# The places of ScalarE's and GpSimd's share in converting the weights, in a fused attention and feed-forward kernel

## The chip, the cores and the metric

The kernel runs on one core of a Trainium2 chip. The core has a matrix engine (TensorE, PE in the profile; its weight loads are PEld), three engines for elementwise work (VectorE or DVE, ScalarE or ACT, GpSimd or POOL), and a queue that issues transfers (SyncE, SP). Each engine works through its own instructions in the order in which the program gives them, and waits for others by semaphores. The metric is the device time of one execution in microseconds (us). Times of several executions are given as a median. One further execution was recorded by the profiler.

## What is computed

```python
def _attn_ref(q, k, v, tau):
    scores = scale * np.matmul(q, k.transpose(0, 1, 3, 2))
    thresh = np.max(scores, axis=-1, keepdims=True) - tau
    scores = np.where(scores >= thresh, scores, -1000000000.0)
    ...
    attn = attn / (np.sum(attn, axis=-1, keepdims=True) + 1e-09)
    return np.matmul(attn, v)
...
    xn = (x - mu) / np.sqrt(var + 1e-06) * g_ln
    ch = np.maximum(xn @ w_ch1, 0.0) @ w_ch2
    return (x + ch)
```

There are 8 batches, 8 heads, 576 positions and 64 features per head. A softmax keeps only the scores within tau of the row's largest. The heads side by side make the 512 features of the second half, a normalisation and a feed-forward network of 2048 hidden features. The two weight matrices, w_ch1 (512 x 2048) and w_ch2 (2048 x 512), arrive as 64-bit floating point numbers, while q, k and v are 32-bit. Converting those weights on the chip is what the change is about.

## The kernel before

**Attention.** The work goes in 72 stages (n), nine per batch. Stage n takes two heads with half of their 512 first queries, or, in the fifth stage of a batch, the 64 last queries of all heads. It makes four blocks of 128 queries by 576 keys: the scores on PE (L422, into sc), their row maxima on DVE (L436), exponentials on ACT (L450, two pairs, one per half of sc), and on DVE the product with the mask (score at least threshold), which also sums the rows (L457). The reciprocal of these sums (L464, L462) is applied in one of two ways. In stages 0 to 5 ACT writes it into diagonal matrices (L471), and PE multiplies the blocks by them and turns them in the same step (tp, tr), which ACT copies out (L507, L501, L530). From stage 6 on (FIRST) POOL scales the blocks (L473), DVE turns them by 32 x 32 blocks into et (L547), and two transfers through memory (scr, L554; em, L568) put them in place. PE then multiplies by the values (L616, L626), and ACT copies the result to x (L639). In stages 1 to 4 PE is also given some products of constants (warm) ahead of the scores.

**Feed-forward.** Each batch gives two groups of 288 tokens. A group's first layer has 16 steps d: 16 matmul records of 128 x 288 into one of two banks of PSUM in turn, then ACT's relu (L814), which frees the bank. Group 0 runs its second layer plainly; its matmuls appear as p at L101, as those of the first layer do. Later groups use a scheme with seven products for eight (seg). The generator of these steps is drawn on by second_part, four times in a stage, so that PE's order is attention and feed-forward in fixed alternation.

**The conversion.** The weights are cut into 32 chunks of 128 x 512: 0 to 15 are w_ch1, four for each quarter of the hidden features, and 16 to 31 are w_ch2. A chunk is fetched raw (two 32-bit words for a number) into a free place. Then
- begin (DVE, L273 and L277) takes sign, exponent and upper mantissa from the upper word into the chunk;
- ScalarE converts the lower word to its top bits (here called the convert, L283), and squares the upper word, taken as a 32-bit number, in place (the square, L286). The square overwrites what begin reads;
- carry (POOL, L296) adds the converted word to the chunk as an integer;
- mask (DVE, L302) compares the square with a constant and multiplies the chunk by the result; it frees the raw place;
- scale (POOL, L312) multiplies a chunk of w_ch1 by g_ln.

A step of the first layer needs the four scaled chunks of its quarter, one of the second layer the masked chunk.

**What sets the order.** It is written out by hand in the loop over n. The table BEGUN says how many chunks shall have been begun at three places of stage n: at masks_at (after the second pair of exponentials), at behind_at (after the L457s) and at end_at (at the end of the stage). In stages 1 to 5 two places are used: one chunk is begun at masks_at and one at end_at. From stage 6 on two or three are begun at masks_at and as many at behind_at. The two ScalarE operations of a chunk are put on one list, on_scalar, by begin, as a pair. They are given to ACT by flush: all at once in carry_all, or one after each relu of the first layer. mask_all masks every carried chunk; it is called ahead of the begins at masks_at and ahead of those at behind_at. The lines of the loop that matter, shortened (next(rest, None) gives the second pair of exponentials):

```python
        next(rest, None)
        ...
        conversion.mask_all()
        conversion.begin_to(masks_at)
        if n <= HP + 1:
            conversion.carry_all()
            conversion.scale_all()
        run(n, 1)
        second_part(n, 1)
        conversion.carry_all()
        conversion.scale_all()
        ...
        diags = weights(es, thr, blocks_go)
```

Of the kernel before, what the change touches and what calls it, by code (L numbers as in the profile page):

```python
# [13 lines left out]
AF = mybir.ActivationFunctionType  # L14
# [4 lines left out]
def kernel(  # L19
# [31 lines left out]
    nc = tc.nc  # L51
# [4 lines left out]
    HP = H // 2  # L56
# [120 lines left out]
    class Weights:  # L177
# [13 lines left out]
        def __init__(self):  # L191
            self.chunks = [
                (w1_sb[i][:, c : c + WC], w_ch1[i * 128 : (i + 1) * 128, c : c + WC], i)
                for c in range(0, DF, WC)
                for i in range(NK)
            ] + [
                (
                    w2_sb[:, m, d : d + 4].rearrange("p d c -> p (d c)"),
                    w_ch2[d * 128 : (d + 4) * 128, m * 128 : (m + 1) * 128].rearrange(
                        "(d p) c -> p d c", p=128  # L200
                    ),
                    None,
                )
                for m in range(NK)
                for d in range(0, ND, 4)
            ]
            self.n1 = NK * (DF // WC)
            self.fetched = self.begun = self.carried = self.masked = self.scaled = 0
            self.raw, self.ticks, self.on_scalar = {}, 2, []
            flat = lambda t: t.rearrange("p a b -> p (a b)")  # L210

            x_room = ffn.tile([128, NK, TOK], F32, tag="x", bufs=3, name="x_room")
            y_room = ffn.tile([128, NK, TOK], F32, tag="sq", bufs=1, name="y_room")
            stage = self.stage = consts.tile([128, 8, WC], F32, name="stage")

            n1 = self.n1
            self.free = []  # L220
            for t, n, before in (
                (w2_sb.rearrange("p m d c -> p (m d) c"), ND // 2, lambda p: n1 + 2 * p - 6),
                (hidden, 4, lambda p: 10),
                (x_room, 1, lambda p: 2 * n1),
                (y_room, 1, lambda p: 2 * n1),
                (stage, 4, lambda p: 2 * n1),
            ):
                for p in range(n):
                    self.free.append((before(p), -1, flat(t)[:, p * 2 * WC : (p + 1) * 2 * WC]))
# [15 lines left out]
        def fetch(self, most=99, wait=1):  # L245

            while self.fetched < len(self.chunks) and most:
                i = self.fetched
                got = self.piece(i, wait)
                if got is None:  # L250
                    break
                most -= 1
                self.fetched += 1
                self.raw[i] = got
                _, src, gi = self.chunks[i]
                raw = got[2].bitcast(I64)
                nc.sync.dma_start(
                    out=raw if gi is not None else raw.rearrange("p (d c) -> p d c", d=4), in_=src
                )
# [7 lines left out]
        def begin(self):  # L267
            i = self.begun
            assert all(self.raw[j][0] + 6 > i or self.raw[j][0] == 10 for j in range(self.masked, i))
            self.begun += 1  # L270
            hi = self.words(i, U32)[:, :, 1]
            au = self.chunks[i][0].bitcast(U32)
            nc.vector.tensor_scalar(  # L273
                out=au, in0=hi, scalar1=3, scalar2=0x3FFFFFFF,
                op0=ALU.logical_shift_left, op1=ALU.bitwise_and,
            )
            nc.vector.scalar_tensor_tensor(  # L277
                out=au, in0=hi, scalar=0xC0000000, in1=au,
                op0=ALU.bitwise_and, op1=ALU.bitwise_or,
            )  # L280
            low, low_in, top = self.words(i, I32), self.words(i, U32), self.words(i, F32)[:, :, 1]
            self.on_scalar += [
                lambda: nc.scalar.activation(  # L283
                    low[:, :, 0], low_in[:, :, 0], func=AF.Copy, scale=2.0**-29
                ),
                lambda: nc.scalar.activation(top, top, func=AF.Square),  # L286
            ]

        def flush(self, most=99):
            while self.on_scalar and most:  # L290
                most -= 1
                self.on_scalar.pop(0)()

        def carry(self, i):
            ai = self.chunks[i][0].bitcast(I32)
# [34 lines left out]
        def carry_all(self):  # L330


            self.flush()
            for i in reversed(range(self.carried, self.begun)):
                self.carry(i)
            self.carried = self.begun

        def mask_all(self):
            while self.masked < self.carried:
                self.mask()  # L340

# [4 lines left out]
    FIRST = HP + 2  # L346

    def by_blocks(n):

        return n >= FIRST  # L350
# [370 lines left out]
    def run_all(calls):  # L721
        now = calls[:]
        calls.clear()
        for fn in now:
            fn()
# [68 lines left out]
    def first_part(g):  # L794


        xc = centred.pop(g)
        rb = sq = None
        plain = g == 0
        sums_of = differences() if g == 1 else iter(())  # L800
        for d in range(ND):
            while conversion.ended < 4 * (d // 4 + 1):
                yield 0, 0
            while d == ND - 2 and len(rooted) <= g:
                run_all(aside)
            p1 = ps_ff.tile([128, TOK], F32, tag="ff", name="p1")
            for c in range(NK):
                product(
                    p1, lhsT=w1_sb[c][:, d * 128 : (d + 1) * 128], rhs=xc[:, c],
                    start=(c == 0), stop=(c == NK - 1),  # L810
                )
                if c < NK - 1:
                    yield 1, 1
            nc.scalar.activation(hidden[:, d], p1, func=AF.Relu)  # L814
            conversion.flush(1)
            next(sums_of, None)
            yield 2, 1
            if sq is None and d and (plain or part > 1 or d == ND // 2 - 1):
                squared = d
                sq = hidden[:, ND - NK :]  # L820
                nc.scalar.activation(sq, xc, func=AF.Square)  # L821
                for c in range(1, NK):
                    nc.gpsimd.tensor_tensor(out=sq[:, 0], in0=sq[:, 0], in1=sq[:, c], op=ALU.add)  # L823
            elif sq is not None and rb is None and (
                d >= squared + (7 if plain else 3) and part > (0 if plain else 1)
                or d == ND - NK - 1
            ):
                var = ps_ff.tile([128, TOK], F32, tag="ff", name="var")
                product(var, lhsT=avg_sb, rhs=sq[:, 0], start=True, stop=True)
                rb = ffn.tile([128, TOK], F32, tag="rb", bufs=2, name="rb")  # L830
                nc.scalar.activation(sq[:, 2], var, func=AF.Identity, bias=eps_sb)
                nc.scalar.activation(rb, sq[:, 2], func=AF.Ln)
                nc.scalar.activation(rb, rb, func=AF.Exp, scale=-0.5)
                aside.append(lambda: root(rb, sq[:, 2], sq[:, 3]))
                yield 1, 1
        for _ in sums_of:
            pass
        return rb
# [168 lines left out]
    def at_quarter(n, i, fn, *args):  # L1007
        later_calls.setdefault((n, i), []).append((fn, args))
# [52 lines left out]
    conversion = Weights()  # L1061
# [31 lines left out]
    for n in range(NS):  # L1093
# [33 lines left out]
            run_all(aside)  # L1127
        conversion.mask_all()
        conversion.begin_to(masks_at)
        if n <= HP + 1:  # L1130
            conversion.carry_all()
            conversion.scale_all()
        run(n, 1)
        second_part(n, 1)
        conversion.carry_all()
        conversion.scale_all()
        blocks_go = by_blocks(n)
        diags = weights(es, thr, blocks_go)
        run_all(aside)
# [1 line left out]
        if n < SLOTS:  # L1141
            run_all(stores)
        conversion.mask_all()
        conversion.begin_to(behind_at)
        run(n, 2)
        second_part(n, 2)
        conversion.carry_all()
        box = []
        if blocks_go:
            conversion.fetch(3, wait=0)  # L1150
            scr = turn_blocks(b, s, es)
            at_quarter(n + 1, 0, lambda b=b, s=s, scr=scr, box=box: box.append(fetch(b, s, scr)))
        else:

            made = turn_weights(s, es, diags)
            for i, at in enumerate(
                (-1, -1, 0, 0)
            ):
                if i < 3:
                    at_quarter(n + 1, at, next, made)  # L1160
                else:
                    at_quarter(n + 1, at, lambda made=made, box=box: box.append(next(made)))
# [62 lines left out]
```

## Times and profile before

| what | value |
|---|---|
| median of 3 runs | 1353.67 us (1351.93 to 1353.77) |
| the profiled execution | 1355.44 us |
| its span from first to last instruction | 1353.6 us |
| granted PE clock, mean | 0.995 of full speed |
| distance of the ends of the scores, stages 2 to 6 | 11.06, 11.07, 10.62 and 10.64 us |
| last mask of a weight chunk | 171.5 us |

A profile's page gives busy times, then the span in slices, the chain of work that ended last, the costliest groups of instructions, and the transfers. Other views used here are the queue of one engine in order of time and the busy times by stretch. In a row of a queue stand the start, the duration, the engine, the line and operation, what is written and read (buffer numbers left out, so that all chunks of the first matrix are w and a raw place is called by the tile in which it lies: w, hidden, stage, x_room, y_room or e), how many instructions the row merges, and in brackets the idle time ahead of it with what ended it. PE's durations are modelled, so its records overlap a little.

### The profile page before, as it was taken

How to read it: one execution, taken by the hardware profiler on the slowest of the kernel's cores; microseconds unless marked ns; L12 is line 12 of the kernel's file. 1: busy time of each engine (PE TensorE's matmuls, PEld its weight loads, DVE VectorE, ACT ScalarE, POOL GpSimd, SP SyncE). 2: the span in 40 equal slices, each digit the busy share in tenths (PEclk: the TensorE clock that was granted, in tenths of full speed). 3: DMA queues.
4: the chain of work that ended last, by engine and by line, in shares of the span. 5: the costliest groups of instructions: out<-in, count | busy, mean ns of one | idle time of the engine just before them, and what ended most of it. 6: DMA issues, size and time to landing. Idle time of an engine off the chain costs nothing.

```text
span 1353.6 us, 40455 instructions
## 1 busy us (share of the span) xinstructions
PE 1320.4 (98%) x17400; PEld 993.8 (73%) x17400; DVE 877.9 (65%) x1544; ACT 458.8 (34%) x995; POOL 630.3 (47%) x836
## 2 busy tenths in 40 slices
PE   8989899999999999999999999999999999999997
PEld 6754557869687786967778696876868677686957
DVE  7979977666755675666766667556756667666112
ACT  4865432232323323232333323233232323323120
POOL 3566655445444344444534545444444445335312
PEclk9999999999999999999999999999999999999999
DMA  8916884457644675437744476446764376343211
GB/s 159 290 39 185 216 210 148 176 155 188 182 146 146 191 194 174 151 129 192 194 141 159 138 199 182 151 146 186 188 181 152 119 195 185 125 159 128 85 18 20
DMA packets 335299, 213.94 MB, mean 158 GB/s; under 512 B 247376, under 2 KB 292688, under 8 KB 327056
## 3 DMA queue, kind: packets, MB, share of 16 engines
q1 hardware_dynamic: 329008, 210.46, 53.3%
q8 instruction: 137, 2.24, 0.7%
q10 hardware_dynamic: 5952, 0.74, 0.4%
q0 software_dynamic: 160, 0.15, 0.1%
q14 instruction: 42, 0.34, 0.1%
HBM read 124.00 MB, written 87.29 MB: 156 GB/s over the span
## 4 chain that ended last, share of the span: by engine, by line
PE 87%; SPq 1%; issue 1%; DMA 1%; DVE 0%; POOL 0%; ACT 0%; POOLq 0%; ACTq 0%; DVEq 0%
PE p L101 36%; PE seg L101 31%; PE sc L422 9%; PE sc L616 8%; PE sc L626 2%; PE var L101 1%; PE mean L101 1%; DMA em<-scr 0%; SPq L554 0%; ACT part L902 0%; SPq L118 0%; DMA k_in<-in_k_dram 0%; DVE et L547 0%; POOL w L296 0%; POOL out_dram L745 0%
## 5 line engine op out<-in xcount | busy, mean ns | idle before, releaser
L101 PE MATMUL p<-xc,w 128*64 128x288 f32 x4096 | 519.4, 409 | 9.8 <-ACT part L902 4.6
L101 PEld LDWEIGHTS p<-xc,w 128*64 128x64 f32 x4096 | 287.2, 137 | 219.6 <-issue 14.8
L436 DVE TENSOR_REDUCE neg<-sc 128x2 f32<-128x1152 f32 x144 | 188.6, 1351 | 282.4 <-PE sc L422 282.4
L473 POOL TENSOR_SCALAR e<-e,den 128x576 f32<-128x576 f32 x264 | 209.5, 805 | 133.6 <-DVE den L462 133.6
L101 PE MATMUL seg<-hidden,w 128*64 128x144 f32 x3840 | 247.9, 287 | 0.0
L101 PEld LDWEIGHTS seg<-hidden,w 128*64 128x64 f32 x3840 | 234.9, 137 | 11.5 <-issue 8.5
L457 DVE SCALAR_TENSOR_TENSOR e<-sc,thr,e 128x576 f32<-128x576 f32 x288 | 222.3, 809 | 17.3 <-POOL thr L440 11.6
L440 POOL TENSOR_SCALAR thr<-neg,low_sb 128x2 f32<-128x2 f32 x144 | 41.6, 289 | 377.7 <-DVE neg L436 376.8
L814 ACT ACTIVATE hidden<-p 128x288 f32<-128x288 f32 x256 | 106.2, 415 | 295.6 <-PE p L101 295.6
L450 ACT ACTIVATE e<-sc,neg 128x576 f32<-128x576 f32 x288 | 197.5, 754 | 2.4 <-DVE neg L436 2.4
L547 DVE STREAM_TRANSPOSE et<-e 128x1152 f32<-128x1152 f32 x118 | 161.1, 1372 | 14.3 <-POOL e L473 13.7
L422 PE MATMUL sc<-kT,qT 64*64 64x384 f32 (+3 forms) x2048 | 139.4, 403 | 3.1 <-DVE e L457 1.9
L616 PE MATMUL sc<-em,v_in 128*64 128x128 f32 (+1 forms) x2368 | 130.9, 264 | 5.2 <-DMA em<-scr 3.7
L616 PEld LDWEIGHTS sc<-em,v_in 128*64 128x64 f32 x2368 | 123.4, 138 | 14.0 <-DVE o L728 2.5
L101 PE MATMUL seg<-hidden,stage 128*64 128x144 f32 x1920 | 123.3, 286 | 0.0
L101 PEld LDWEIGHTS seg<-hidden,stage 128*64 128x64 f32 x1920 | 117.6, 137 | 2.9 <-issue 2.9
L639 ACT COPY x<-sc 128x128 f32<-128x128 f32 x120 | 31.6, 265 | 243.8 <-PE sc L422 176.0
L887 POOL TENSOR_TENSOR hidden<-hidden 128x576 f32<-128x576 f32 x60 | 84.8, 1428 | 52.0 <-ACT hidden L814 42.4
L422 PEld LDWEIGHTS sc<-kT,qT 64*64 64x64 f32 x2048 | 76.0, 133 | 44.2 <-issue 21.4
L902 ACT COPY part<-seg 128x288 f32<-128x288 f32 x74 | 29.8, 403 | 190.6 <-PE seg L101 190.1
L887 DVE TENSOR_TENSOR hidden<-hidden 128x576 f32<-128x576 f32 x60 | 51.2, 887 | 51.5 <-PE seg L101 48.5
L823 POOL TENSOR_TENSOR hidden<-hidden 128x288 f32<-128x288 f32 x48 | 38.9, 810 | 54.7 <-ACT hidden L821 52.2
(132 smaller groups left out, 1088.2 us busy)
## 6 DMA issues: line engine op xcount, KB each, us to landing
scr<-et SPq DMA_DIRECT2D x63, 1152.0 KB, 5.0
em<-scr SPq DMA_DIRECT2D x63, 1024.0 KB, 5.7
out_dram<-ot SPq DMA_DIRECT2D x248, 36.0 KB, 3.6
q_in<-in_q_dram SPq DMA_DIRECT2D x120, 72.0 KB, 2.5
er<-scr SPq DMA_DIRECT2D x132, 64.0 KB, 5.1
k_in<-in_k_dram SPq DMA_DIRECT2D x116, 72.0 KB, 2.8
v_in<-in_v_dram SPq DMA_DIRECT2D x28, 256.0 KB, 5.4
w<-in_moe_w_ch_dram SPq DMA_DIRECT2D x11, 512.0 KB, 6.5
```

What stands on the lines that cost most here:

```text
L101: nc.tensor.matmul(out[r], lhsT=lhsT[:, r], rhs=rhs, **flags)
L422: nc.tensor.matmul(sc[h][64 * i : 64 * i + 64, at : at + n], lhsT=ql[r] if s == HP else qT[r, half, j * 128 + 64 * i : j * 128 + 64 * i + 64],
L436: nc.vector.tensor_reduce(out=neg[:, i], in_=pairs[h], axis=AXL.X, op=ALU.max, negate=True,)
L440: nc.gpsimd.tensor_scalar(out=thr[:, i], in0=neg[:, i], scalar1=-1.0, scalar2=low_sb, op0=ALU.mult, op1=ALU.add,)
L450: nc.scalar.activation(es[:, i], blocks[i], func=AF.Exp, bias=neg[:, i : i + 1])
L457: nc.vector.scalar_tensor_tensor(out=es[:, i], in0=blocks[i], scalar=thr[:, i : i + 1], in1=es[:, i], op0=ALU.is_ge, op1=ALU.mult, accum_o ...
L473: nc.gpsimd.tensor_scalar(out=es[:, i], in0=es[:, i], scalar1=den[:, i : i + 1], scalar2=1.0, op0=ALU.mult, op1=ALU.mult,)
L547: nc.vector.transpose(et[:, :, 64 * h : 64 * h + 64].rearrange("p n (j c) -> p j n c", j=2), es[:, 2 * h : 2 * h + 2].rearrange("p j (n c) ...
L616: nc.tensor.matmul(dst[64 * h : 64 * h + 64], lhsT=vt[:, h, c, :], rhs=pick(em[:, 2 * j : 2 * j + 2, c], h), start=c == 0 and first, stop= ...
L814: nc.scalar.activation(hidden[:, d], p1, func=AF.Relu)
L823: nc.gpsimd.tensor_tensor(out=sq[:, 0], in0=sq[:, 0], in1=sq[:, c], op=ALU.add)
L887: eng.tensor_tensor(out=out[at], in0=in0[at], in1=in1[at], op=op)
```

## The change

The list on_scalar becomes two: lows (the converts) and squares. give_scalar hands out a list's calls. carry_all now gives the converts only. The squares are given at mask_all, after second_part(n, 1), after the carries behind the L457s, and one after each relu in place of an operation of the old list. In the loop, carry_all and scale_all at masks_at run in every stage, ahead of second_part(n, 1). From stage 6 on the scales of the chunks masked behind the L457s are given there, and not in the next stage; the carries of the chunks begun at behind_at are given after the turning of the blocks (turn_blocks), with the converts ahead of it and the squares left over between.

```diff
-            self.raw, self.ticks, self.on_scalar = {}, 2, []
+            self.raw, self.ticks, self.lows, self.squares = {}, 2, [], []
...
-            self.on_scalar += [
-                lambda: nc.scalar.activation(
-                    low[:, :, 0], low_in[:, :, 0], func=AF.Copy, scale=2.0**-29
-                ),
-                lambda: nc.scalar.activation(top, top, func=AF.Square),
-            ]
-
-        def flush(self, most=99):
-            while self.on_scalar and most:
+            self.lows.append(lambda: nc.scalar.activation(
+                low[:, :, 0], low_in[:, :, 0], func=AF.Copy, scale=2.0**-29
+            ))
+            self.squares.append(lambda: nc.scalar.activation(top, top, func=AF.Square))
+
+        def give_scalar(self, calls, most=99):
+            while calls and most:
                 most -= 1
-                self.on_scalar.pop(0)()
+                calls.pop(0)()
...
         def carry_all(self):
-            self.flush()
+            self.give_scalar(self.lows)
...
         def mask_all(self):
+            self.give_scalar(self.squares)
             while self.masked < self.carried:
...
             nc.scalar.activation(hidden[:, d], p1, func=AF.Relu)
-            conversion.flush(1)
+            conversion.give_scalar(conversion.squares, 1)
...
         conversion.mask_all()
         conversion.begin_to(masks_at)
-        if n <= HP + 1:
-            conversion.carry_all()
-            conversion.scale_all()
+        conversion.carry_all()
+        conversion.scale_all()
         run(n, 1)
         second_part(n, 1)
-        conversion.carry_all()
-        conversion.scale_all()
+        conversion.give_scalar(conversion.squares)
         blocks_go = by_blocks(n)
         diags = weights(es, thr, blocks_go)
...
         conversion.mask_all()
+        if n >= FIRST:
+            conversion.scale_all()
         conversion.begin_to(behind_at)
         run(n, 2)
         second_part(n, 2)
-        conversion.carry_all()
+        conversion.give_scalar(conversion.lows)
+        if n < FIRST:
+            conversion.carry_all()
+            conversion.give_scalar(conversion.squares)
         box = []
         if blocks_go:
             conversion.fetch(3, wait=0)
             scr = turn_blocks(b, s, es)
+            conversion.give_scalar(conversion.squares)
+            conversion.carry_all()
```

## Prediction

> **What bounds the kernel now.** I read the page's busy times first, then the busy times by stretch, then the queues of ScalarE (ACT), VectorE (DVE) and TensorE (PE) in order of time. The page says PE, and over the whole span that is right:
>
> ```profile
> PE 1320.4 (98%) x17400; PEld 993.8 (73%) x17400; DVE 877.9 (65%) x1544; ACT 458.8 (34%) x995; POOL 630.3 (47%) x836
> ```
>
> The conversion of the weights, which is all that the change touches, ends at 172 us. There the table of stretches says something else (columns: stretch, its length, busy PE, PEld, DVE, ACT, POOL, granted clock, DMA share, GB/s):
>
> ```profile
> 25.00:50.00 25.00, 23.06 (x380) 19.30 (x376) 24.32 (x47) 19.28 (x41) 12.05 (x15) 1.00 0.94 216
> 50.00:75.00 25.00, 23.17 (x410) 18.37 (x406) 22.60 (x41) 20.94 (x49) 15.27 (x16) 1.00 0.89 296
> ...
> 125.00:150.00 25.00, 21.52 (x198) 12.57 (x196) 23.11 (x37) 11.89 (x23) 17.00 (x16) 0.93 0.72 180
> ...
> 200.00:225.00 25.00, 25.00 (x284) 15.84 (x282) 19.00 (x32) 6.62 (x17) 12.88 (x15) 1.00 0.52 165
> ```
>
> From 25 to 75 us DVE is full and ACT nearly; from 200 us PE has no gap. PE's order is fixed, so a microsecond that PE waits before 180 us is a microsecond of the end. Stage 2 shows the early chain. ACT's queue by time:
>
> ```profile
> 36.18 1.08 ACT L507 COPY em<-tp 128x512 f32<-128x512 f32 x2
> 37.59 0.37 ACT L530 COPY er<-tr 128x256 f32<-128x256 f32 x1 [0.33 <-PE tr L521]
> 37.85 1.38 ACT L450 ACTIVATE e<-sc,neg 128x576 f32<-128x576 f32 x2
> 39.11 0.69 ACT L283 ACTIVATE hidden<-hidden 128x512 int32<-128x512 uint32 x1
> ```
>
> and DVE's in the same stretch:
>
> ```profile
> 36.15 0.65 DVE L302 SCALAR_TENSOR_TENSOR w<-hidden,w 128x512 f32<-128x512 f32 x1
> 36.72 0.41 DVE L273 TENSOR_SCALAR w<-hidden 128x512 uint32<-128x512 uint32 x1
> 37.17 0.69 DVE L277 SCALAR_TENSOR_TENSOR w<-hidden,w 128x512 uint32<-128x512 uint32 x1
> 37.78 0.81 DVE L457 SCALAR_TENSOR_TENSOR e<-sc,thr,e 128x576 f32<-128x576 f32 x1
> ...
> 40.08 0.81 DVE L457 SCALAR_TENSOR_TENSOR e<-sc,thr,e 128x576 f32<-128x576 f32 x1
> ```
>
> The reader is to see the order: the mask (L302) stands ahead of the begin (L273, L277) and of the four L457, and runs before the second pair of exponentials (L450 at 37.85) has begun. PE waits for the last L457 with the next scores (L422). Later, PE's own stalls are few and dear:
>
> ```profile
> 96.50 1.63 PE L101 MATMUL p<-xc,w 128*64 128x288 f32 x12
> 100.58 3.65 PE L101 MATMUL p<-xc,w 128*64 128x288 f32 x16 [2.46 <-ACT hidden L814]
> ...
> 124.63 4.35 PE L101 MATMUL p<-xc,w 128*64 128x288 f32 x32
> 131.00 10.15 PE L101 MATMUL p<-hidden,w 128*64 128x288 f32 x68 [2.02 <-ACT hidden L814]
> ```
>
> [...] the relu of 100.14 stood 6.48 us behind a square that waited for a begin. [...] after 2.46 us (100.58), 2.02 us (131.00) and 3.75 us with four matmuls within (165.28) the clock reads 0.50 for 3.4 to 3.9 us, which costs 1.7 (16 matmuls in 3.65 us where 123 ns each would be 1.96), 1.8 and 1.9 us; after 1.43 us (142.80) it stays 1.00. [...] the mask takes 0.65 us alone and 1.17 us at 41.23, beside a POOL scale.
>
> **What moves.** The two kernels' instruction orders, laid side by side, are equal on PE, DVE and SP, so no DMA issue moves. Only ACT's and POOL's differ; nothing is added or removed. (convert: L283, square: L286, carry: L296, scale: L312.)
>
> **1: squares behind the exponentials, stages 1 to 6.** A square used to stand right behind its convert, at a stage's end. Now convert stays, and the square of the chunk begun last waits for the next stage's mask_all, which is behind both pairs of exponentials. In stage 2 ACT gives: convert, em, em, exp, exp, em, em, er, exp, exp, square. DVE's order did not move, so its mask waits for that square, and behind it wait the begin, the four L457, the diagonals and the next scores. Let S be the start of a stage's last scores (30.34 in stage 2).
> - ACT comes free behind the exponentials at 39.11, S+8.77; square 0.69: S+9.46; mask S+9.5 (before: 36.15, S+5.8).
> - Mask to first L457 took 1.63 us (36.15 to 37.78), first to end of last L457 3.11 (to 40.89), scores 0.07 later: the next S is S+14.3.
> - Scores ended at 32.50, 43.56, 54.63, 65.25, 75.89: periods 11.06, 11.07, 10.62, 10.64. At 14.3 each: 3.24+3.23+3.68+3.66 = 13.8 us.
> - Stage 1 has two squares there: behind exponentials that free ACT at 26.32, they end at 26.99 and 27.55; first mask at 27.0 in place of 25.00, second at 27.6: with the begin, L457 starts at 29.24 in place of 27.25, and scores shift by 2.1 us.
>
> Sum 15.9 us. What it gives back: em copies no longer wait up to 1.0 us behind a square (44.04), but the second em copy waits for PE (0.23 at 45.51), so nothing; taken as 0. The warm matmuls fill 1.9 us per stage in 1 to 4, and PE still stands some 3.2 us (S+11.1 to S+14.3, with only four matmuls within) there, nearly 5 us ahead of scores 5 and 6. POOL's carry of the chunk behind ends at S+12.5, ahead of its mask at S+14.5. Fetches wait for raw buffers that masks give back, so they start up to 3.7 us later in their stage; the DMA share of 0.01 between 75 and 100 us says that all had landed by then, so that hides.
>
> **2: the clock.** No such gap occurs there now, so the cost is bounded: 0 [...] to 5 x 1.9 = 9.5 us. Below zero is excluded: a gap speeds nothing. I take four of five at 1.8: 7.2 us.
>
> **3: stage 6** (its times as in the trace of before; add the shift). The square of chunk 11 stands behind the first relu (84.30): mask at 85.3 instead of 80.10, L457 over at 92.3 instead of 87.1. Cover: POOL now carries chunks 12 to 14 ahead of the three additions of xc's squares, from 89.2, all seven over at 96.2 where 96.42 was: POOL's e (L473) starts as before. The next masks come at 93.0 instead of 95.27, begin 15 ends at 96.4 instead of 99.5. But the hook after a relu now gives squares alone, so the square of 15 stands behind the fourth relu, not the fifth, and waits for begin 15; the fifth relu (d4) comes at 96.5, and PE's d6 waits from 93.9 to 96.9, with a slow clock. Then 5.7 us of matmuls and 1.7 of clock: 104.3; before, 104.17. Net +0.1.
>
> **4: stage 7.** Converts 18 and 19 move ahead of var's chain (1.15 us): d10 +0.8. POOL's scales 12 to 14 and carry 18, 19 come 1.5 us sooner, which takes away the 0.47 us wait at 117.5. Again a square moves one relu up: 20's behind d10's relu. Begin 20 ends at 122 (three L755 to L759 operations and two masks before it, stretched by POOL). So d11's relu is at 122.7 and d13 stands from 118.7 to 123.1, then runs slow: scores 8 end at 131 instead of 124.7. The 2.02 us stall of 131.00 and its 1.8 us vanish, as exponentials are not late for relus any more; the second layer starts at 134.8 at full clock, against 131.0 + 1.8. Net +2.0.
>
> **5: stages 8, 9.** Reductions 8 start at 131 instead of 127.75; with three masks, three begins and the turning, L457 ends 2.5 us later. Converts 23 to 25 before all squares give 0.4 us to the carries; carries behind the turning free POOL for nothing that waits. Turning 8 ends 1.9 us late (152.0), the em fetch that PE awaits at 165.28 lands 1.8 us late. PE is bound from there on: 4's loss is within this, in all +1.8 (bounds -4, if begin 15 and 20 come earlier than I think, and +6).
>
> **Sum.** 15.9 + 7.2 + 1.8 = 24.9. The profiled run took 1355.44 (span 1353.6, 1.84 around it): 1380.3. That is 1.77 over the median of the three runs, 1353.67, for which I give 1378.5.
>
> **Rivals.**
> - No slow clock early, or part given back later: 1353.7 + 15.9 - 4 to + 1.8: 1365.6 to 1371.4. [...] Against: 2.02 us sufficed. 20%.
> - Worse: all five slow and stage 7's stall carried to the end (+6): 1353.7 + 15.9 + 9.5 + 6 = 1385. For: d13's 4.4 us stall is the longest in sight. Against: the scores' slack. 10%.
> - Faster: the relus' two stalls with their clock (2.46+1.7, 2.02+1.8 = 8.0) vanish, and the early squares are covered: 1345.7. It decides if the masks wait less than 1.6 us a stage (8.0 over five), which needs the square by S+7.4. Against: ACT is not free before S+8.77, and the relus get a square ahead of them earlier, not later. 5%.
> - No difference: the two cancel, or DVE's order hides the mask: 3%.
>
> The forecast (1371.4 to 1385) has 62%. The range, 1365 to 1386, takes in the first two rivals: its ends are the early sum with 4 given back and no slow clock, and all at its worst. A measurement of this kernel tells about 0.2% (2.7 us) from no change: faster 5%, same 3%, slower 92%.
>
> **What would show it.** DVE idle some 3.5 us before L302 in stages 2 to 5, released by ACT's square; scores ending 14 to 16 us apart; PEclk below 1 before 100 us; d13's stall for a relu; PE without gaps from about 205 us. I am wrong if the masks don't wait in stages 1 to 5, if the period stays near 11, or if the part after the first p matmul shortens by over 10 us.

## The result, and the profile after

| what | before | after |
|---|---|---|
| median | 1353.51 us (1351.93 to 1353.77, 4 runs) | 1384.36 us (1384.04 to 1385.09, 4 runs) |
| ratio, 95% interval | | 1.0231 (1.0213 to 1.0249) |
| the profiled execution | 1355.44 us | 1384.62 us |
| its span | 1353.6 us | 1382.2 us |
| granted PE clock, mean | 0.995 | 0.986 |
| ends of the scores, stages 2 to 6 (us) | 32.50, 43.56, 54.63, 65.25, 75.89 | 34.71, 50.48, 64.95, 81.22, 97.65 |
| start of scores 7, 8, 9, 10 (us) | 104.58, 122.58, 146.69, 170.84 | 129.97, 154.76, 173.62, 199.58 |

The changed kernel is slower by 30.85 us by the medians and by 28.6 us by the spans. I had forecast 24.9, so the measured time lies near the upper edge of what I gave (1371.4 to 1385) and close to the rival "worse" (1385); the time alone does not tell the two apart, the traces do. The kernel before ran its profiled execution 1.9 us above its median and the changed one 0.3 us, which is most of the difference between the two figures; the rest, 0.6 us, lies outside the span.

Lines of the changed kernel are called by its own numbers here: convert L282, square L285, carry L294, mask L300, scale L310, scores L421, exponentials L449, product with the mask L456, the diagonals' reciprocal L463, POOL's scaling of blocks L472, relu L813, the additions of xc's squares L822. The page of the changed kernel, its line of busy times:

```profile
PE 1330.2 (96%) x17400; PEld 999.9 (72%) x17400; DVE 875.8 (63%) x1544; ACT 459.7 (33%) x995; POOL 624.8 (45%) x836
```

DVE, ACT and POOL had as many instructions as before, and their busy times differ by 0.9 us (ACT) to 5.5 us (POOL). PE's busy time grew by 9.8 us with the same 17400 records, at a mean granted clock of 0.986 in place of 0.995; the other 19 us of the span are idle. The table of stretches (stretch, its length, busy PE, PEld, DVE, ACT, POOL, clock, DMA share, GB/s) says where:

```profile
25.00:50.00 25.00, 19.32 (x280) 14.82 (x276) 17.93 (x38) 15.20 (x33) 9.55 (x12) 0.95 0.83 206
50.00:75.00 25.00, 18.62 (x292) 15.35 (x288) 14.03 (x25) 16.18 (x33) 7.27 (x12) 0.98 0.69 226
75.00:100.00 25.00, 20.40 (x258) 13.37 (x260) 15.64 (x29) 11.60 (x27) 10.65 (x19) 0.73 0.27 86
```

From 25 to 75 us DVE was nearly full before (24.32 and 22.60 of 25 us); now it is busy for 17.93 and 14.03, and no engine is full. That is the sign of a queue that waits for another engine and holds up what stands behind it. In stage 2 the queue of ACT by time shows the order that the change made:

```profile
40.07 1.38 ACT L449 ACTIVATE e<-sc,neg 128x576 f32<-128x576 f32 x2
41.33 0.69 ACT L285 ACTIVATE hidden<-hidden 128x512 f32<-128x512 f32 x1
```

and the queue of DVE shows who pays for it:

```profile
42.05 0.69 DVE L300 SCALAR_TENSOR_TENSOR w<-hidden,w 128x512 f32<-128x512 f32 x1 [3.60 <-ACT hidden L285]
42.65 0.42 DVE L273 TENSOR_SCALAR w<-hidden 128x512 uint32<-128x512 uint32 x1
43.11 0.69 DVE L277 SCALAR_TENSOR_TENSOR w<-hidden,w 128x512 uint32<-128x512 uint32 x1
43.72 0.81 DVE L456 SCALAR_TENSOR_TENSOR e<-sc,thr,e 128x576 f32<-128x576 f32 x1
```

The bracket on L300 is the whole first part of the case: DVE stood idle for 3.60 us until the square of 41.33 was done, although the first pair of exponentials, which the first L456 needs, had ended at 38.52. Over the early stages the table of waits (waiting line, what it waited for: us in total, times, longest us) adds this up, from 16 to 106 us:

```profile
PE sc L421 <- DVE e L456: 14.9, 9, 3.5
DVE w L300 <- ACT w L285: 13.3, 3, 5.7
...
DVE w L300 <- ACT hidden L285: 9.3, 2, 5.7
```

The two rows of L300 are 22.6 us together. Then the queue of PE, the rows with a stall, and two without a slow clock for comparison:

```profile
46.81 3.67 PE L421 MATMUL sc<-kT,qT 64*64 64x384 f32 x28 [0.61 <-DVE e L456]
...
62.79 2.16 PE L421 MATMUL sc<-kT,q_last 64*64 64x384 f32 x28 [0.61 <-DVE e L456]
...
92.07 5.58 PE L421 MATMUL sc<-kT,qT 64*64 64x384 f32 x32 [3.37 <-DVE e L456]
...
122.15 1.23 PE L101 MATMUL p<-xc,w 128*64 128x288 f32 x4 [6.03 <-ACT hidden L813]
148.35 1.23 PE L101 MATMUL p<-xc,w 128*64 128x288 f32 x4 [4.11 <-ACT hidden L813]
160.74 8.41 PE L101 MATMUL p<-hidden,w 128*64 128x288 f32 x68
```

The same 28 score matmuls take 2.16 us at full clock and 3.67 where the clock was halved for part of them (it read 0.50 from 47.29 to 50.71 us). At 122.15 d6 has waited for the fifth relu of stage 6, at 148.35 d13 for one of stage 7. At 160.74 the second layer begins without the 2.02 us stall that it had before. The scores of stage 10 start 28.7 us later than before, and later scores, at 411, 710 and 1012 us of the kernel before, 28.5 us later: behind stage 10 nothing more is lost.

### The profile page after: what moved, and what is told of

Its sections match the earlier page's. It is cut to its first block, busy times and chain, and to the rows that moved or that the text cites. A ratio compares the mean times of both kernels' runs of the same rounds, so it can differ in the third digit from the quotient of the medians.

```text
span 1382.2 us, 40443 instructions
## 1 busy us (share of the span) xinstructions
PE 1330.2 (96%) x17400; PEld 999.9 (72%) x17400; DVE 875.8 (63%) x1544; ACT 459.7 (33%) x995; POOL 624.8 (45%) x836
## 4 chain that ended last, share of the span: by engine, by line
PE 89%; DVE 5%; ACT 2%; issue 1%; SPq 1%; POOL 1%; DMA 1%; POOLq 0%; ACTq 0%; DVEq 0%
PE p L101 36%; PE seg L101 30%; PE sc L421 10%; PE sc L615 8%; PE sc L625 2%; DVE e L456 2%; DVE w L300 1%; ACT e L449 1%; PE tp L101 1%; DVE w L277 1%; POOL w L294 1%; SPq L553 1%; PE var L101 1%; PE mean L101 1%; ACT em L506 0%
## 5 line engine op out<-in xcount | busy, mean ns | idle before, releaser
L472 POOL TENSOR_SCALAR e<-e,den 128x576 f32<-128x576 f32 x264 | 208.8, 803 | 133.1 <-DVE den L461 133.1
L456 DVE SCALAR_TENSOR_TENSOR e<-sc,thr,e 128x576 f32<-128x576 f32 x288 | 222.0, 809 | 14.9 <-POOL thr L439 11.6
L813 ACT ACTIVATE hidden<-p 128x288 f32<-128x288 f32 x256 | 106.4, 416 | 300.2 <-PE p L101 300.2
L449 ACT ACTIVATE e<-sc,neg 128x576 f32<-128x576 f32 x288 | 197.4, 753 | 2.4 <-DVE neg L435 2.4
L421 PE MATMUL sc<-kT,qT 64*64 64x384 f32 (+3 forms) x2048 | 146.9, 415 | 13.2 <-DVE e L456 12.5
L615 PE MATMUL sc<-em,v_in 128*64 128x128 f32 (+1 forms) x2368 | 134.4, 268 | 4.4 <-DVE w L300 2.4
L615 PEld LDWEIGHTS sc<-em,v_in 128*64 128x64 f32 x2368 | 127.0, 140 | 13.7 <-DVE w L300 2.6
L421 PEld LDWEIGHTS sc<-kT,qT 64*64 64x64 f32 x2048 | 78.7, 136 | 58.3 <-issue 23.3
L101 PE MATMUL seg<-hidden,e 128*64 128x144 f32 x896 | 61.2, 286 | 0.0
```

The source lines that it names most:

```text
L101: nc.tensor.matmul(out[r], lhsT=lhsT[:, r], rhs=rhs, **flags)
L421: nc.tensor.matmul(sc[h][64 * i : 64 * i + 64, at : at + n], lhsT=ql[r] if s == HP else qT[r, half, j * 128 + 64 * i : j * 128 + 64 * i + 64],
L449: nc.scalar.activation(es[:, i], blocks[i], func=AF.Exp, bias=neg[:, i : i + 1])
L456: nc.vector.scalar_tensor_tensor(out=es[:, i], in0=blocks[i], scalar=thr[:, i : i + 1], in1=es[:, i], op0=ALU.is_ge, op1=ALU.mult, accum_o ...
L472: nc.gpsimd.tensor_scalar(out=es[:, i], in0=es[:, i], scalar1=den[:, i : i + 1], scalar2=1.0, op0=ALU.mult, op1=ALU.mult,)
L615: nc.tensor.matmul(dst[64 * h : 64 * h + 64], lhsT=vt[:, h, c, :], rhs=pick(em[:, 2 * j : 2 * j + 2, c], h), start=c == 0 and first, stop= ...
```

## The experiments

My theory has three terms. First, a square that stands behind the exponentials makes the masks late, and DVE's queue hands the delay to L456 and to the next scores. Second, the gaps that this leaves in PE slow its clock. Third, from stage 6 on a square that waits for a begin is put one relu earlier than before, so that a relu stands behind it. The rivals: the early loss comes from the other moves on ACT and POOL (converts, carries) and not from the squares; the clock costs nothing that the wait had not cost already; the late loss comes from POOL's new order (carries ahead of the additions), not from the relus.

### One part undone: the early squares back behind their converts

On the changed kernel:

```diff
         conversion.begin_to(end_at)
         conversion.carry_all()
+        if n < FIRST:
+            conversion.give_scalar(conversion.squares)
```

> The change, but with the square of the chunk begun last given at the end of stages 0 to 5 right behind its convert, as before; everything from stage 6 on stays changed, except that the square of chunk 11 is then already done. Theory (late squares hold the masks of stages 1 to 6, and the gaps they make slow PE's clock): the 21.8 us that the scores of stage 6 came late are gone, and some of stage 6's extra 3.6 us with them; DVE doesn't wait for a square ahead of a mask in stages 1 to 5; scores of stages 2 to 6 end 10.6 to 11.1 us apart, PEclk is 1.00 up to 100 us; 1359 to 1363 us. Rival (the moved carries, scales and relu squares from stage 6 on make the loss, and the early stages only carry it): less than 8 us gained, above 1376 us.

Measured: 1360.75 us (1358.87 to 1361.28) against 1353.57 for the kernel before, measured beside it, ratio 1.0054 (1.0039 to 1.0069). The scores of stages 2 to 6 end at 32.49, 43.56, 54.63, 65.25 and 75.89 us, those of the kernel before to 0.01 us. So the place of the squares is all of the early loss; converts and carries have no share in it. What remains, 7.2 us, is the late part. (The first slow row of PE starts at 98.93 us, sooner than the 100 us that I expected, because the late stalls now come that soon: its four matmuls take 1.23 us, and four of the same at full clock 0.66, at 209.66 us.) PE's two large stalls stand in its queue:

```profile
98.93 1.23 PE L101 MATMUL p<-xc,w 128*64 128x288 f32 x4 [5.04 <-ACT hidden L813]
125.84 1.23 PE L101 MATMUL p<-xc,w 128*64 128x288 f32 x4 [4.13 <-ACT hidden L813]
```

### The early part alone

On the kernel before; the rest of the old list stays as it was, pairs and relus:

```diff
-                lambda: nc.scalar.activation(top, top, func=AF.Square),
             ]
+            (self.squares if in_early() else self.on_scalar).append(
+                lambda: nc.scalar.activation(top, top, func=AF.Square)
+            )
...
         def mask_all(self):
+            self.give_squares()
...
         second_part(n, 1)
+        conversion.give_squares()
         conversion.carry_all()
```

Here in_early() is n < FIRST, and give_squares gives the list squares out.

> The kernel before with only the squares of chunks begun in stages 0 to 5 split off and given where the change gives them (at mask_all, behind the second exponentials, or behind second_part(n, 1)); all from stage 6 on as before. Theory: the scores of stage 6 end about 21.8 us later than before, with two to four slow clock episodes up to 100 us, and stages 6 to 9 add 0 to 3 us for the late mask of chunk 11: 1374 to 1379 us. Rival (the late part makes the loss): within 6 us of before, below 1360 us.

Measured: 1378.19 us (1377.38 to 1380.64), ratio 1.0189 (1.0173 to 1.0204): +24.6 us. The scores end at 35.29, 50.88, 65.52, 81.79 and 98.33 us, the pattern of the changed kernel (0.4 to 0.7 us later). With the late part alone, +7.2, this makes 31.8 where 30.85 was measured; by the spans, 22.4 and 5.6 make 28.0 where 28.6 was measured. So the two parts hardly touch each other.

### The masks out of the early stages' first place

On the changed kernel the mask_all ahead of the begin at masks_at is left out in stages 1 to 5; the other mask_all, behind the L456s, then masks two chunks. As mask_all also gives the squares, the late square moves back once more, behind second_part(n, 1) and its convert:

```diff
-        conversion.mask_all()
+        if not 0 < n < FIRST:
+            conversion.mask_all()
         conversion.begin_to(masks_at)
```

> The change with the masks that stand ahead of the begins and of the four L456 in stages 1 to 5 moved behind these L456 on DVE (the first mask_all of these stages left out); the squares stay late. Theory (what costs is that a mask waiting for a late square stands ahead of the L456 in DVE's queue): scores of stages 2 to 6 end 10.5 to 11.5 us apart, no slow clock before 100 us, 20 to 23 us gained, stage 6 on as in the changed kernel: 1361 to 1366 us. Rival (the square's or convert's later place on ACT holds the diagonals or the em copies): periods stay above 13 us, 1378 us or more.

Measured: 1363.39 us (1361.57 to 1363.46), ratio 1.0073 (1.0058 to 1.0088). The scores end at 33.21, 44.65, 55.72, 66.34 and 76.99 us, periods of 10.6 to 11.4 us, with the squares still behind the exponentials (in stage 2 at 40.80 us, behind the convert of 39.83). So a late square by itself costs little (2.6 us against the first experiment); it is dear because the mask that waits for it stands ahead of L456 in DVE's queue. This is the first term shown from its other side.

### The gaps filled: what the clock costs

On the changed kernel PE gets more products of constants ahead of the scores of stages 2 to 6, 192 matmul records more in all. They compute nothing that is used.

```diff
-        if 0 < n <= HP:
-            constants(8 if n > 1 else 26)
+        if 0 < n <= FIRST:
+            constants((26, 16, 14, 14, 14, 14)[n - 1])
```

> The change with more products of constants ahead of the scores of stages 2 to 6 (16, 14, 14, 14, 14 in place of 8, 8, 8, 0, 0), which fill most of the time in which PE waits for L456; nothing else moves. Theory (the gaps slow the clock, and periods of 15.8 to 16.4 us are 14.3 plus that): PEclk 1.00 up to 100 us, periods all 14.2 to 14.5 us, 5 to 6 us gained, 1378 to 1380 us. Rival (the longer periods come from DVE or ACT): periods as in the changed kernel, 1383 to 1386 us, or later if the products stand in the way.

Measured: 1379.89 us (1378.99 to 1382.83), ratio 1.0205 (1.0188 to 1.0223). The stretch from 75 to 100 us, whose clock read 0.73, and two rows of the scores:

```profile
75.00:100.00 25.00, 21.95 (x366) 17.12 (x368) 15.55 (x29) 16.20 (x35) 9.15 (x17) 1.00 0.22 68
```

```profile
74.08 0.86 PE L421 MATMUL sc<-kT,qT 64*64 64x384 f32 x4 [0.42 <-DVE e L456]
75.55 2.16 PE L421 MATMUL sc<-kT,qT 64*64 64x384 f32 x28 [0.61 <-DVE e L456]
```

The clock is at 1.00 in each stretch from 25 to 100 us, and the distances of the scores' ends are 14.27, 14.34, 14.33 and 14.40 us: the 14.3 that the prediction had worked out for the waits alone. Stage 6's scores end at 92.11 instead of 97.65. So the rival falls that the clock costs nothing of its own: the second term is 5.5 us at this place, 5.6 in the span and 4.5 by the medians (26.3 above its kernel before instead of 30.85).

### The relus freed of squares

On the changed kernel, with the early squares put back as in the first experiment:

```diff
             nc.scalar.activation(hidden[:, d], p1, func=AF.Relu)
-            conversion.give_scalar(conversion.squares, 1)
```

> The first experiment's kernel (early squares beside their converts) with no square given behind a relu: in stages 6 and 7 the squares of chunks 15 to 17 and 20 to 22 then stand behind the three relus and the converts. Theory (the stalls of 5.0 and 4.1 us at d6 and d13 are relus behind squares that wait for begins): both stalls and their slow clock vanish, scores 7 start 6 to 7 us earlier than in the first experiment (about 101 us), then DVE, which turns stage 6's blocks until 103 us, limits: in all 3 to 4 us under the kernel before, 1348 to 1352 us. Rival (the relus wait for PE or DVE for another reason, or the squares, now later, hold the masks of these chunks): as the first experiment, 1358 to 1362 us.

Measured: 1349.53 us (1348.57 to 1351.71) against 1353.63 beside it, ratio 0.9971 (0.9959 to 0.9982). Both large stalls are gone; what is left of PE's waits for relus, by its queue:

```profile
106.49 2.16 PE L101 MATMUL p<-xc,w 128*64 128x288 f32 x16 [1.95 <-ACT hidden L813]
...
127.66 7.74 PE L101 MATMUL p<-hidden,w 128*64 128x288 f32 x62 [1.85 <-ACT hidden L813]
```

This is 11.2 us less than the first experiment's 1360.75 for taking one call away, and POOL's order at the place in dispute is the same in both: three carries, a scale, the three additions, the blocks. DVE's three masks there take 3.60 us, against 3.58 in the first experiment. So the third term is right in this, and its rival falls: it is the square ahead of the relu, not POOL's order by itself, that makes PE wait. That the change put this square one relu earlier (behind the fourth instead of the fifth) is read from ACT's queues, shown further below; a kernel that differs in this alone was not run. This kernel is also 4.1 us (0.3%) faster than the kernel before, with the interval clear of 1. Scores 7 start at 99.77 us, 7.7 us earlier than in the first experiment, where 6 to 7 were expected.

### The same call taken out of the kernel before

On the kernel before:

```diff
             nc.scalar.activation(hidden[:, d], p1, func=AF.Relu)
-            conversion.flush(1)
```

> The kernel before with no conversion given behind a relu (converts and squares in their old pairs, all in carry_all). Theory: the stall of 2.46 us at d7 goes with its slow clock; DVE, full from 100 to 165 us, gives back part of it: 1 to 4 us under before, 1349.5 to 1352.5 us. Rival (relus are not held by squares there): 1353 to 1354.5 us.

Measured: 1351.75 us (1350.47 to 1353.45, 16 runs), ratio 0.9987 (0.998 to 0.9995). The stall of 2.46 us is gone, but others take part of its place:

```profile
104.62 2.16 PE L101 MATMUL p<-xc,w 128*64 128x288 f32 x16 [1.01 <-ACT hidden L814]
109.28 7.50 PE L101 MATMUL p<-xc,w 128*64 128x288 f32 x60 [2.01 <-ACT hidden L814]
```

So 1.9 of the 4.1 us that the previous experiment gained on the kernel before are to be had from the kernel before alone. The other 2.2 us come with the change's late part (squares apart from converts, converts and scales sooner) once no relu stands behind a square. Which of its moves brings them stays open; no run took them one by one.

### POOL's additions out of the masks' way

On the changed kernel the three additions of xc's squares (group 0) are given three steps d later, behind the scaling of the blocks and the scales of chunks 12 to 14:

```diff
+    def add_squares(sq):
+        for c in range(1, NK):
+            nc.gpsimd.tensor_tensor(out=sq[:, 0], in0=sq[:, 0], in1=sq[:, c], op=ALU.add)
...
                 nc.scalar.activation(sq, xc, func=AF.Square)
-                for c in range(1, NK):
-                    nc.gpsimd.tensor_tensor(out=sq[:, 0], in0=sq[:, 0], in1=sq[:, c], op=ALU.add)
+                if not plain:
+                    add_squares(sq)
+            elif plain and sq is not None and d == squared + 3:
+                add_squares(sq)
```

> The change with POOL's three additions of xc's squares of group 0 put behind the scales of chunks 12 to 14 instead of ahead of L472; nothing else moves. Theory (in stage 6 the masks of 12 to 14 and begin 15 were slow, 3.57 us for three masks where I reckoned 1.8, because POOL's two-operand additions ran beside them): the three masks take 2.0 to 2.6 us, begin 15 ends 1 to 1.6 us sooner behind the start of the masks, d6's stall falls from 6.0 to about 4.7 us; 1 to 2 us gained, 1382 to 1383.5 us. Rival (the masks' length comes from DVE itself, or from L472 just as well): three masks still 3.3 us or more, stall 6.0, within 0.5 us of the changed kernel.

Measured: 1383.94 us (1383.19 to 1384.47), ratio 1.0224 (1.021 to 1.0238), 0.4 us better than the changed kernel by the medians. The rows of DVE and POOL in question:

```profile
114.86 2.85 DVE L300 SCALAR_TENSOR_TENSOR w<-w,w 128x512 f32<-128x512 f32 x3 [0.65 <-POOL w L294]
```

```profile
115.46 5.92 POOL L472 TENSOR_SCALAR e<-e,den 128x576 f32<-128x576 f32 x4
```

The masks take 2.85 us in place of 3.57 (2.0 to 2.6 expected), from their start to the end of begin 15 it is 4.25 us in place of 5.66, and the stall of d6 is 4.63 us in place of 6.03. So POOL's additions did stretch the masks and the begin, and this is a part of the stall. But the blocks' scaling, which now lies beside the masks, stretches them too (three in a row took 1.9 us in the first experiment, at 112.15), and takes 5.92 us itself in place of 4.87. In time it is inconclusive: 0.4 us is less than can be told apart, and less than the 1 to 2 us expected. The profiled execution has a span 1.5 us shorter, but 0.6 us of this was there already at the end of stage 6's scores (97.1 instead of 97.65), ahead of all that the edit moves: the slow clock's episodes in the early stages fell differently in this execution.

### Both together

The edits of the two experiments "relus freed of squares" and "additions out of the masks' way" on one kernel: early squares back, no squares at relus, additions later.

> Early squares beside their converts, no square behind a relu, and POOL's additions later: the version to which the experiments point. Theory: as the one without relu squares, and up to 1.5 us less, because stage 6's turning ends sooner: 1347 to 1351.5 us. Rival (the additions hide anyway once the relus are free): the same as that one within 0.5 us.

Measured: 1349.72 us (1349.53 to 1350.27), ratio 0.9971 (0.9959 to 0.9982), the same as without the additions moved (1349.53); so the rival held, and nothing of the 1.5 us was gained. Once no relu stands behind the begins, the stretched masks delay nothing that PE waits for.

## Why the prediction was right, and where a term was off

**Step 1, squares behind the exponentials, was right in kind and size.** It said that the next scores start 14.3 us after the last, 15.9 us in all. With the clock held up (fourth experiment) the periods are 14.27 to 14.40, stage 1's shift is 2.2 us where 2.1 was worked out, and the scores of stage 6 end 16.2 us late. (One reading ahead of it was too strong: ACT, called nearly full from 25 to 75 us, was busy for 19.28 and 20.94 of 25 us. Nothing rests on it, since the order counts here and not the idle time.) The first two experiments give it from both sides, and the third shows the link in DVE's queue.

**Step 2, the clock, was a bound, and its middle was a little high.** Of the five gaps three slowed the clock, not four: it was halved from 47.3 to 50.7, 74.6 to 81.4 and 91.7 to 98.5 us. They cost 5.5 us by the fourth experiment, where 7.2 was taken (0 to 9.5 the range, its lower end an estimate of mine), so each cost about 1.8 in the mean, as assumed, and it was their number that was off (another 0.4 us of slow clock falls into step 3). Which gaps are slowed is not fixed by the kernel: the run with the additions later, which differs only from stage 6 on, slowed the scores of stages 2, 5 and 6 (rows of 3.53, 3.71 and 5.58 us), the changed kernel those of 3, 5 and 6 (3.67, 5.58 and 5.58). That the guess of four came so near is in part luck. (The 3.4 to 3.9 us that the prediction read for a slow stretch of the kernel before are 3.41 us each, by finer stretches.) Both together: 23.1 predicted, 21.8 measured at the end of stage 6's scores.

**Step 3, stage 6, was the mis-sized term.** The prediction had +0.1 us between the scores of stages 6 and 7; the traces have +3.6 (28.69 us from the end of the one to the start of the next before, 32.32 after). The mechanism was named: the square of chunk 15 stands behind the fourth relu, not the fifth, and waits for begin 15. The size was not: the prediction let masks 12 to 14 start at 93.0, begin 15 end at 96.4 (of these 3.4 us 1.8 for the masks, as the expectation of the experiment with the additions says) and d6 go on at 96.9, after a stall of 3.0. In the prediction's times (less the 21.8 us shift) the masks began at 93.7, begin 15 ended at 99.3, and d6 went on at 100.4, after 6.0. ACT's queue before, where the square stands behind the fifth relu of the stage and the sixth waits:

```profile
92.68 0.40 ACT L814 ACTIVATE hidden<-p 128x288 f32<-128x288 f32 x1
99.56 0.68 ACT L286 ACTIVATE w<-w 128x512 f32<-128x512 f32 x1 [6.48 <-DVE w L277]
100.14 0.40 ACT L814 ACTIVATE hidden<-p 128x288 f32<-128x288 f32 x1
```

The kernel before, DVE's queue at this place:

```profile
95.27 2.31 DVE L302 SCALAR_TENSOR_TENSOR w<-w,w 128x512 f32<-128x512 f32 x3 [7.95 <-POOL w L296]
```

After, DVE's queue:

```profile
115.44 3.57 DVE L300 SCALAR_TENSOR_TENSOR w<-w,w 128x512 f32<-128x512 f32 x3 [0.64 <-POOL w L294]
118.94 1.01 DVE L273 TENSOR_SCALAR w<-w 128x512 uint32<-128x512 uint32 x1
119.98 1.12 DVE L277 SCALAR_TENSOR_TENSOR w<-w,w 128x512 uint32<-128x512 uint32 x1
```

POOL's queue beside it:

```profile
116.05 3.61 POOL L822 TENSOR_TENSOR hidden<-hidden 128x288 f32<-128x288 f32 x3
119.65 4.87 POOL L472 TENSOR_SCALAR e<-e,den 128x576 f32<-128x576 f32 x4
```

and ACT's queue, where the first row is the fourth relu and the last is the fifth, for which d6 waits:

```profile
113.50 0.40 ACT L813 ACTIVATE hidden<-p 128x288 f32<-128x288 f32 x1
121.13 0.68 ACT L285 ACTIVATE w<-w 128x512 f32<-128x512 f32 x1 [7.23 <-DVE w L277]
121.71 0.39 ACT L813 ACTIVATE hidden<-p 128x288 f32<-128x288 f32 x1
```

The reader is to see that the carries ahead of POOL's three additions, which I had entered as a gain (masks from 93.0 instead of 95.27), put the additions beside the masks. Each mask took 1.19 us in place of the 0.65 of one alone (0.77 at this place before), and the additions 3.61 us in place of 2.56. So d6 went on 3.5 us later than reckoned. Begin 15 ended 2.9 us late: 0.7 by a later start, 1.7 in the masks, 0.6 in the begin. Of the later start 0.4 us is the clock of step 2, still slow until 98.5 us at the head of the stage (the first p matmul 6.57 us behind the scores' end, 6.14 before and also in the fourth experiment). The last 0.6 us is a slip of the sum: from the end of begin 15 to PE it is 1.05 us in both kernels (99.53 to 100.58 before, 121.10 to 122.15 after), as the square and then the relu have to run, and the prediction left the square out and took 0.5. The prediction had a single mask at 1.17 us beside a POOL scale and at 0.65 us alone; these three took as long, beside the additions. I had priced stage 7's masks as stretched by POOL, and not stage 6's, although the step itself moved POOL's work there. The experiment with the additions put later confirms a part of it (2.85 us, a stall of 4.63). No run took the whole stretch away.

**Step 4, stage 7, was right.** d13 stood 4.11 us where 4.4 was worked out, d10 waited 0.64 where 0.8 was; the scores of stages 7 and 8 are 6.8 us further apart, where 131 in place of 124.7 had meant 6.3. The stall at the second layer and its slow clock went as predicted (68 matmuls in 8.41 us in place of 10.15), and this layer starts 2.6 us late against scores 7, with 1.8 us of clock saved counted in, where 2.0 was said.

**Step 5, stages 8 and 9, was short by 1.6 us.** From scores 7 on the final shift grows from 25.4 to 28.7 us, 3.3 where 1.8 all in all was taken. The scores of stage 9 stand 26.9 us late, those of stage 10 28.7. The prediction let PE's waits of stage 9 absorb what stage 7 had lost; they did not, and stage 9 added 1.8 us of its own. In its trace 1.25 us is a new wait of the second layer's matmuls for a mask of the second matrix (at 186.36). This wait is in the trace of every run that keeps the late part with its squares at the relus (1.26 us at 164.22 in the first experiment), and in none of the others, so it goes with them; how it arises was not traced further. The slow clock at 194.1 to 197.5 us is no new loss: the kernel before has one as long at the same place (165.9 to 169.4), and the 44 matmuls there take 5.6 us in both.

**The sum.** The errors partly cancel: 24.9, less 1.3 early, plus 3.5 in stage 6, plus 1.6 behind it, is 28.7, the shift at stage 10 (28.6 at the end, by the spans). Another 0.6 us lies outside the span, and 1.7 us come of the profiled execution before being above its median by more than the one after (1.9 and 0.3): 30.9 worked out, 30.85 measured. Of the rivals, "no slow clock early" falls by the fourth experiment. "Worse" was right that the clock and the late stalls would both count, and wrong in their places: three slow gaps early, not five, and the excess in stage 6, not in stage 7's stall. "Faster" needed the square 7.4 us into a stage; ACT gave it at 9.5, as worked out.

## What to carry to other kernels

An instruction moved back on one engine is not priced by its own idle time there. Follow the queue of the engine that waits for it: here 0.69 us of ACT work, given behind the exponentials, made DVE stand 3.60 us in front of a 0.69 us mask, and all that the mask stands ahead of in DVE's order stood with it. When a helper queue is emptied at fixed places (one call after each relu), a change of what is on it also changes which call each place gives; look for the one call that waits, and who stands behind it. And where a step brings two engines' work side by side that was apart, reprice both rows, not the one that moved.

## What the runs showed of the hardware that was not expected

- Between 16 and 215 us PE's granted clock read 0.50 six times in the trace of the changed kernel (47.29 to 50.71, 74.60 to 81.43, 91.67 to 98.49, 118.97 to 125.80, 146.28 to 153.11 and 194.07 to 197.48 us) and three times in that of the kernel before (101.09 to 104.50, 131.81 to 135.22 and 165.94 to 169.36 us), else 1.00. Within each of the two traces all these falls and rises lie a whole number of 3.413 us from each other, to 0.01 us.
- In the 3.41 us ahead of each of the nine falls PE was busy for 0.45 to 1.40 us by its records, so it had not stood idle for all of them. With 1.65 us idle, four matmuls and 0.61 us idle (45.33 to 46.81 us of the changed kernel) PE was busy for 1.34 of the 3.41 us up to 47.29, and the clock fell there; with 1.73 and 0.61 us idle (61.31 to 62.79) it was busy for 2.05 us from 57.53 to 60.94 and 2.44 us from 60.94 to 64.36, and the clock stayed at 1.00.
- Of the six slow stretches of the changed kernel two lasted 3.41 us, and PE was busy all through them. Four lasted 6.83 us, at gaps of 3.4 to 6.0 us; PE was busy for 0.24 to 3.01 us of their first 3.41 us, and for all of the second.
- DVE and POOL both took longer side by side: POOL's three additions 3.61 us beside masks (changed kernel, 116.05) and 2.56 us with DVE idle (kernel before, 87.72), the masks 1.19 us each there and 0.65 us with POOL idle (kernel before, 36.15), and four scalings of blocks 5.92 us beside masks and begins (additions later, 115.46) and 4.87 us beside begins alone (changed kernel, 119.65).
